# The Gram products of a later block, run directly behind the outputs of the delta rule

## The chip, the core and the metric

The kernel runs on one core of one Trainium2 chip. The metric is the device time of one execution in microseconds; smaller is better. The engines named below are PE (TensorE: matmuls, with PEld for its weight loads), DVE (VectorE), ACT (ScalarE) and SP (SyncE, which issues nearly all DMAs). Each engine works through its own list of instructions in order and waits at an instruction until what it needs is there.

## The reference

Two stages are fused: a delta-rule attention over 4 sequences, 8 heads, 768 tokens and a head dimension of 48, and an MLP on its output.

```python
k_n = k / (np.linalg.norm(k, axis=-1, keepdims=True) + 1e-06)
for t in range(S):
    y[:, :, t] = np.einsum('bhd,bhde->bhe', q[:, :, t], state)
    v_old = np.einsum('bhde,bhd->bhe', state, kt)
    state = state + bt[:, :, :, None] * np.einsum('bhd,bhe->bhde', kt, vt - v_old)
...
x = y, as 3072 tokens of 8 * 48 = 384 features
h = x @ w_in                      # 384 -> 2048
out = np.maximum(0.01 * h, h) @ w_out   # 2048 -> 384
```

Here `kt`, `vt` and `bt` are the key (normalised), value and step size of token t.

## The kernel before

**Blocks.** The 768 tokens of each sequence are cut into 12 blocks of 64. Inside a block the recurrence is replaced by matrix products and one triangular inverse; only the small state passes from block to block. For a block n there are these parts:

- `gram(n)`: the products of keys with keys and with queries. It loads the operands `kq` (four DMAs on SP, L267), starts the key lengths of the block before (`pn`, L530, copied to `nt` by ACT, L537), and then makes two groups of 16 matmuls each (`pg`, L287). A group fills two PSUM banks, b = 0 and b = 1; the operands of b = 0 lie on partitions 0 to 47, those of b = 1 from 64 on. The source goes through the two banks in alternation. ACT copies the key-key half of each bank to `gs` (L291), SP stores pieces of it to `gd` (L295), DVE masks the key-query half into `rq` (L302) and copies a corner to `gm` (L307), and SP loads `L` from `gd` (L310).
- `inv(n)`: an elimination by rows on DVE (`tmp` L351, `T` L356), some sixty pairs of small instructions per block, then a copy of `T` by ACT (L416), stores and loads through memory (`td`, `tt`, `sq`, `rt`) and the products `pz` and `pu` (L451).
- `solve(n)`: the steps that need the state: `pk` (L575), `pw` (L591), `pc` (L601), which makes the new state, and `py` (L611), whose copy `ys` (L613) is the block's output.
- `ffn(n)`: the MLP on the block's 256 tokens, in 16 f-steps. An f-step makes `ph` (nine matmuls, L670). ACT forms `gh` (L675) and rewrites `ph` in place (L676), DVE takes the difference `gl` (L678), and `po` (L660, six matmuls) of the f-step two before is added up. Two PSUM banks hold `ph`: f-steps of one parity share a bank and change between its halves. Behind the f-steps `columns` transposes the next block's output (`px`, L641) into `xh` and `xl` (L119, L120).

**What runs with what.** MLP block n is interleaved with `solve(n+1)`, `inv(n+2)` and `gram(n+3)`. `weave` goes through the f-steps of a block and calls the other parts' generators in windows of f-steps. The Gram of blocks 5 to 11 has the window 12 to 13: it is called in one piece in f-step 12, in MLP blocks 2 to 8.

**What sets the order.** From this source a scheduler makes one list of instructions per engine. `behind(name)` gives it one more edge: what is issued inside comes after the instruction that was last marked with that name. The products `pg` stand behind "ph". All products of `solve` and `gram` take their PSUM from one pool of four banks, in turn (`ps_a`, L68), so a product waits until the copies out of the bank's last use are done. `kq` has two buffers, one for each of a block's two groups.

Of the kernel before, what the change touches and what calls it, by code (L numbers as in the profile page):

```python
# [25 lines left out]
NGR = NSEQ // GS  # L26
# [5 lines left out]
P = 128  # L32
# [14 lines left out]
def delta_moe_kernel(ctx: ExitStack, tc, kq0, kqT, kv, qT, beta, cst, w_all, out, nblk):  # L47
# [208 lines left out]
            done.add((gram, n))  # L256
            yield

    def gram(n):
        need(sv, solve, n - Q_BUFS // NGR)  # L260
        kqs = []
        for g in range(NGR):
            t = sb.tile([P, GS, NPAIR, 2, C], F32, tag="kq", name=f"kq{n}_{g}", bufs=KQ_BUFS)
            kqs.append(t)
            with behind("kq"):
                for b in range(2):
                    nc.sync.dma_start(t[b * R0:b * R0 + D].rearrange("p s u x t -> p (s u x t)"), kqT[n, g, b])  # L267
        b0 = where[n][0]
        Lh[b0] = sb.tile([P, HC, HC], F32, tag="L", name=f"L{b0}", bufs=2)
        gd = dr.tile([64, HC, HC], F32, tag="gd", name=f"gd{n}")  # L270
        if n - 1 > 1 and where[n - 1][0] in nrm:
            with behind("ph"):
                lengths(n - 1)
        for g in range(NGR):
            kq = kqs[g]
            gs = sb.tile([P, 2, NPAIR, C], F32, tag="gs", name=f"gs{n}_{g}", bufs=2)
            if not g:
                gm[n] = sb.tile([P, GU, HC], F32, tag="gm", name=f"gm{n}", bufs=GM_BUFS)

            ps = [ps_a.tile([P, 512], F32, tag="a", name=f"pg{n}_{g}_{b}") for b in range(2)]  # L280
            pv = [x.rearrange("p (u x t) -> p x u t", u=NPAIR, x=2) for x in ps]
            for p in range(NPAIR):
                for c in range(2):
                    for b in range(2):
                        r = slice(b * R0, b * R0 + D)
                        with behind("ph") if n > 2 else nullcontext():
                            nc.tensor.matmul(ps[b][c * 64:(c + 1) * 64, p * 128:(p + 1) * 128],  # L287
                                             kq[r, c ^ b, p, 0], kq[r, c ^ b, p].rearrange("p x t -> p (x t)"),
                                             start=True, stop=True)
            for b in range(2):  # L290
                nc.scalar.copy(gs[:, b], pv[b][:, 0])  # L291
            for c in range(2):
                for e in range(2):
                    a = e * HS + g * GH + c * GU
                    nc.sync.dma_start(  # L295
                        gd[a:a + GU].rearrange("l j i -> j l i"),
                        gs[c * 64 + e * HC:c * 64 + (e + 1) * HC].rearrange("p b u t -> p (b u) t")[:, :, e * HC:(e + 1) * HC])
            qa = of("q", n, g)
            for b in range(2):
                for c in range(2):  # L300
                    r = slice(c * 64, (c + 1) * 64)
                    nc.vector.tensor_tensor(  # L302
                        qa[DN, c, b * NPAIR:(b + 1) * NPAIR], pv[b][r, 1],
                        tri[r].rearrange("p (o t) -> p o t", o=1).broadcast_to([C, NPAIR, C]), ALU.mult)
            for c in range(2):
                k = 2 * g + c
                nc.vector.tensor_copy(gm[n][k * HC:(k + 1) * HC].rearrange("p (b u) t -> p b u t", b=2), gs[c * 64:c * 64 + HC, :, :, HC:])  # L307
            if g == NGR - 1:
                for r in range(2):
                    nc.sync.dma_start(Lh[b0][r * 64:(r + 1) * 64].rearrange("l j i -> l (j i)"), gd.rearrange("l j i -> l (j i)"))  # L310
                done.add((gram, n))
            yield
# [232 lines left out]
    def solve(n):  # L545
        b = where[n][0]
        need(iv, inv, b)
        if n not in nts:
            with behind("po"):
                lengths(n)  # L550
        nt = nts.pop(n)

        def load(g):
            merge_z(n, g, tv(n, g))
            if n:
                fetch(n, g)

        def tie(g):
            merge_u(n, g, tv(n, g))

        def heads(rows):

            return ((c, u, slice(c * 64, c * 64 + rows)) for u in range(GU) for c in range(2))

        def out_of(x, g, w):
            p = ps_a.tile([P, 512], F32, tag="a", name=f"{x}{n}_{g}")
            return p[:, 0:GU * w].rearrange("p (u t) -> p u t", u=GU)

        def kt(g):

            t, k, v = tv(n, g), of("k", n, g), of("v", n, g)
            if n:
                pv = out_of("pk", g, C)
                for c, u, r in heads(D):
                    nc.tensor.matmul(pv[r, u], k[DN, c, u], t[DN, c, u // NPAIR, u % NPAIR], start=True, stop=True)  # L575
                for c in range(2):
                    nc.scalar.mul(t[UP, c], pv[c * 64:c * 64 + D].rearrange("p (y v) t -> p y v t", y=2), -1.0)  # L577
            if not n:
                return
            for s in range(GS):  # L580
                us = slice(s * NPAIR, (s + 1) * NPAIR)
                with behind("gl"):
                    nc.vector.tensor_tensor(
                        v[DN, :, us], v[DN, :, us],
                        nt[DN, g, :, us].rearrange("p h (u o) -> p h u o", o=1).broadcast_to([C, 2, NPAIR, D]), ALU.mult)

        def step_w(g):
            t, v = tv(n, g), of("v", n, g)
            pv = out_of("pw", g, D)
            for c, u, r in heads(C):  # L590
                nc.tensor.matmul(pv[r, u], t[:, c, u // NPAIR, u % NPAIR], v[:, c, u], start=True, stop=True)  # L591
            for c in range(2):
                d = nc.scalar.copy(v[DN, c], pv[c * 64:c * 64 + C])  # L593
            mark["rv"] = d.ins

        def step_s(g):
            k, v, v1 = of("k", n, g), of("v", n, g), of("v", n + 1, g)
            pv = out_of("pc", g, D)
            for c, u, r in heads(D):
                with nullcontext() if n else behind("px"):  # L600
                    nc.tensor.matmul(pv[r, u], k[:, c, u], v[:, c, u], start=True, stop=True)  # L601
            for c in range(2):
                nc.scalar.copy(v1[UP, c], pv[c * 64:c * 64 + D])  # L603

        def step_y(g):

            qa, v = of("q", n, g), of("v", n, g)
            pv = ps_a.tile([P, 512], F32, tag="a", name=f"py{n}_{g}")
            for c, u, _ in heads(C):
                s = c ^ (u // NPAIR)  # L610
                nc.tensor.matmul(pv[s * C:(s + 1) * C, u * D:(u + 1) * D], qa[:, c, u], v[:, c, u], start=True, stop=True)  # L611
            ys[n, g] = y = sb.tile([P, DO], F32, tag="ys", name=f"ys{n}_{g}", bufs=3)
            mark["ys"] = nc.scalar.copy(y, pv[:, 0:DO]).ins  # L613

        stages = [(0, load), (1, tie), (LD, kt), (LD + 1, step_w), (LD + 2, step_s), (LD + 2, step_y)]
        if n in (0, nblk - 1):
            stages.remove((LD + 2, step_s))
        for s in range(NSLOT):
            for g in range(NGR):
                for at, stage in stages:  # L620
                    if at == s:
                        stage(g)
            if s == NSLOT - 1:
                done.add((solve, n))
                if n == 0:
                    columns(0)
                    yield
                    for g in range(NGR):
                        step_s(g)
            yield  # L630
# [19 lines left out]
    def ffn(n):  # L650
# [5 lines left out]
        def second(f, gh, gl, tiles=range(NTB)):  # L656
            for t in tiles:
                ts_ = slice(t * P, (t + 1) * P)
                for k, (a, w) in enumerate(((gh, wo[0]), (gh, wo[1]), (gl, wo[0]))):
                    i = nc.tensor.matmul(  # L660
                        po[t][:, :DO], a[:, ts_], w[f],
                        start=(f == 0 and k == 0), stop=(f == NFC - 1 and k == 2))
            mark["po"] = i.ins

        for f in range(NFC):
            ph = hbank[f % 2][:, f // 2 % 2]
            k = 0
            for cc in range(NCC):
                for a, e in ((wi[0], 0), (wi[0], 1), (wi[1], 0)):
                    i = nc.tensor.matmul(ph, a[f][:, cc * P:(cc + 1) * P], x[cc][e], start=(k == 0), stop=(k == 3 * NCC - 1))  # L670
                    k += 1
            mark["ph"] = i.ins
            gh = sb.tile([P, TB], F32R, tag="gh", name=f"gh{n}_{f}", bufs=FB)
# [70 lines left out]
    for n in range(nblk):  # L744
# [1 line left out]
        weave(NF, (ff, NF, 0, NF), (wg, NFC * (n == 0), 0, WB),  # L746
              (lw, (NFC - 1) * (n == 0), 1 - LL, NFC - LL), (sv, (NS + (n == 0)) * (n + 1 < nblk), *SV[min(n, 3)]),
              (iv, NI * (n + 2 < nblk), *IV[min(n, 3)]), (gg, NGR * (n < 3), *GG[min(n, 2)]),
              (gg, NGR * (1 < n < nblk - 3), 12, 13))


WAHEAD, WEARLY = 4, 8
# [4 lines left out]
LL, AG = 2, 6  # L757
SV = (0, 9), (3, 11), (2, 11), (2, 11)
PD, FB = 2, 3


def _layout(inputs):
# [62 lines left out]
```

## Time and profile before

| | us |
|---|---|
| median of 3 runs | 645.03 (643.98 to 645.08) |
| profiled execution, its time | 645.91 |
| its span, first to last instruction | 644.1 |
| PE busy | 600.8 |
| DVE busy | 444.5 |
| ACT busy | 332.2 |

A timeline row is: start in us, length in us, engine, line and operation, output and inputs, count, and in brackets the idle time before it with what ended it. A chain row is: start, length, engine, tile and line; the chain is the work that ended last, followed back through what released each step. In a row of a window the length of the stretch is followed by the busy time of PE, PEld, DVE, ACT and POOL with their instruction counts, the granted TensorE clock as a share of full speed, the busy share of the DMA engines and GB/s. Many matmuls of the source are two instructions each in the trace, and a few of their records are missing.

### The profile page before, as it was taken

To read this page: it belongs to the slowest core of one execution; us is meant where nothing else is said; L and a number is where in the kernel's file an instruction comes from. 1 tells how busy PE (TensorE), PEld (TensorE's weight loads), DVE (VectorE), ACT (ScalarE), POOL (GpSimd) and SP (SyncE) were. 2 spreads that over 40 slices of the span, in tenths; PEclk is the share of its full clock that TensorE was granted. 3 is DMA by queue.
4 is the path that set the end of the run, shared out by engine and by line. 5 is a ranking of instruction groups with operands and counts; after the bars stand their busy time and mean duration, and the time that the engine had idled before them with its cause. 6 is when DMAs were issued, how large, how long until landed. Compare 5 with 4: busy or idle time off the path is not lost.

```text
span 644.1 us, 19692 instructions
## 1 busy us (share of the span) xinstructions
PE 600.8 (93%) x7710; PEld 560.3 (87%) x7710; DVE 444.5 (69%) x1996; ACT 332.2 (52%) x856; POOL 10.7 (2%) x17
## 2 busy tenths in 40 slices
PE   4287999989999989999999999999999999999996
PEld 4275888989889888999999999999999999999996
DVE  3999999988645959759749749659669659221221
ACT  3465998524645435635545546545545545444322
POOL 6000000000000000000000000000000000000000
PEclk9987999989999989999999999999999999999999
DMA  4992962153165641561561570660660640400101
GB/s 115 295 261 85 252 234 76 26 108 51 30 126 103 134 98 28 103 120 37 101 110 49 114 139 6 118 138 4 121 135 4 126 81 16 79 16 1 26 1 26
DMA packets 124573, 59.52 MB, mean 92 GB/s; under 512 B 111424, under 2 KB 114624, under 8 KB 124480
## 3 DMA queue, kind: packets, MB, share of 16 engines
q1 hardware_dynamic: 123904, 57.54, 40.5%
q8 instruction: 61, 1.00, 0.6%
q10 hardware_dynamic: 576, 0.72, 0.5%
q14 instruction: 32, 0.26, 0.1%
HBM read 46.96 MB, written 11.27 MB: 90 GB/s over the span
## 4 chain that ended last, share of the span: by engine, by line
PE 80%; DVE 7%; DMA 7%; ACT 4%; issue 2%; DVEq 0%; SPq 0%; ACTq 0%
PE ph L670 32%; PE po L660 30%; PE pk L575 3%; PE pw L591 3%; PE pg L287 3%; PE py L611 3%; PE pc L601 2%; DMA kq<-in_kqT 2%; DMA rv<-in_kv 2%; PE px L641 1%; DMA wr<-in_w_all 1%; DVE cg L151 1%; DVE tmp L351 1%; DVE T L356 1%; DVE rq L302 1%
## 5 line engine op out<-in xcount | busy, mean ns | idle before, releaser
L670 PE MATMUL ph<-xh,w 128*128 128x256 f32 x1152 | 247.5, 290 | 5.4 <-DVE gl L678 4.4
L670 PEld LDWEIGHTS ph<-xh,w 128*128 128x128 f32 x1152 | 192.6, 191 | 14.0 <-DVE gl L678 5.7
L660 PE MATMUL po<-w,gh 128*128 128x384 f32 x768 | 188.0, 343 | 3.2 <-ACT gh L675 3.2
L678 DVE TENSOR_TENSOR gl<-ph,gh 128x256 fp32r<-128x256 f32 x192 | 80.2, 421 | 140.5 <-ACT ph L676 138.3
L670 PE MATMUL ph<-xl,w 128*128 128x256 f32 x576 | 163.0, 284 | 1.0 <-DVE xl L120 1.0
L675 ACT ACTIVATE gh<-ph 128x256 fp32r<-128x256 f32 x192 | 73.7, 384 | 170.8 <-PE ph L670 169.0
L660 PEld LDWEIGHTS po<-w,gh 128*128 128x128 f32 x768 | 133.4, 189 | 8.1 <-ACT gh L675 5.3
L660 PE MATMUL po<-w,gl 128*128 128x384 f32 x384 | 115.2, 340 | 0.0
L351 DVE TENSOR_TENSOR tmp<-T,L 128x60 f32<-128x60 f32 (+35 forms) x661 | 112.4, 207 | 0.9
L356 DVE TENSOR_TENSOR T<-T,tmp 128x60 f32<-128x60 f32 (+35 forms) x661 | 111.9, 207 | 0.9
L670 PEld LDWEIGHTS ph<-xl,w 128*128 128x128 f32 x576 | 109.9, 191 | 1.8 <-DVE xl L120 1.5
L676 ACT ACTIVATE ph<-ph 128x256 f32<-128x256 f32 x192 | 73.2, 381 | 0.0
L660 PEld LDWEIGHTS po<-w,gl 128*128 128x128 f32 x384 | 66.8, 190 | 0.1
L302 DVE TENSOR_TENSOR rq<-pg,csb 64x256 f32<-64x256 f32 x80 | 33.8, 423 | 12.6 <-ACT gs L291 11.3
L593 ACT COPY rv<-pw 64x384 f32<-64x384 f32 x48 | 22.7, 473 | 17.9 <-PE pw L591 17.1
L577 ACT ACTIVATE rt<-pk 48x512 f32<-48x512 f32 x44 | 26.1, 592 | 10.0 <-PE pk L575 9.3
L603 ACT COPY rv<-pc 48x384 f32<-48x384 f32 x44 | 20.8, 474 | 13.8 <-PE pc L601 13.5
L591 PEld LDWEIGHTS pw<-rv,rt 128*64 128x64 f32 x768 | 25.1, 145 | 3.1 <-ACT ph L676 2.3
L611 PE MATMUL py<-rv,rq 128*64 128x48 f32 x768 | 27.6, 227 | 0.0
L591 PE MATMUL pw<-rv,rt 128*64 128x48 f32 x768 | 26.8, 230 | 0.0
L120 DVE TENSOR_TENSOR xl<-px,xh 128x256 fp32r<-128x256 f32 x36 | 14.2, 419 | 17.8 <-ACT xh L119 17.8
L611 PEld LDWEIGHTS py<-rv,rq 128*64 128x64 f32 x768 | 25.7, 143 | 0.2 <-ACT ph L676 0.2
(96 smaller groups left out, 557.5 us busy)
## 6 DMA issues: line engine op xcount, KB each, us to landing
wr<-in_w_all SPq DMA_DIRECT2D x16, 768.0 KB, 7.6
kq<-in_kqT SPq DMA_DIRECT2D x40, 192.0 KB, 5.1
L<-gd SPq DMA_DIRECT2D x20, 256.0 KB, 4.0
rk<-in_kv SPq DMA_DIRECT2D x24, 192.0 KB, 3.7
rv<-in_kv SPq DMA_DIRECT2D x24, 192.0 KB, 4.6
rq<-in_qT SPq DMA_DIRECT2D x24, 192.0 KB, 4.5
out<-ob SPq DMA_DIRECT2D x46, 96.0 KB, 2.9
gd<-gs SPq DMA_DIRECT2D x80, 32.0 KB, 2.0
```

The costliest lines, as they stand in the source:

```text
L302: nc.vector.tensor_tensor(qa[DN, c, b * NPAIR:(b + 1) * NPAIR], pv[b][r, 1], tri[r].rearrange("p (o t) -> p o t", o=1).broadcast_to([C, NP ...
L351: nc.vector.tensor_tensor(tv, t[:, :, j:j + 1].broadcast_to([P, k, w]), L[:, j, j + 1:].rearrange("p (o w) -> p o w", o=1).broadcast_to([P ...
L356: mark["steps"] = nc.vector.tensor_tensor(t, t, tv, ALU.subtract).ins
L577: nc.scalar.mul(t[UP, c], pv[c * 64:c * 64 + D].rearrange("p (y v) t -> p y v t", y=2), -1.0)
L591: nc.tensor.matmul(pv[r, u], t[:, c, u // NPAIR, u % NPAIR], v[:, c, u], start=True, stop=True)
L593: d = nc.scalar.copy(v[DN, c], pv[c * 64:c * 64 + C])
L611: nc.tensor.matmul(pv[s * C:(s + 1) * C, u * D:(u + 1) * D], qa[:, c, u], v[:, c, u], start=True, stop=True)
L660: i = nc.tensor.matmul(po[t][:, :DO], a[:, ts_], w[f], start=(f == 0 and k == 0), stop=(f == NFC - 1 and k == 2))
L670: i = nc.tensor.matmul(ph, a[f][:, cc * P:(cc + 1) * P], x[cc][e], start=(k == 0), stop=(k == 3 * NCC - 1))
L675: nc.scalar.activation(gh, ph, AF.Prelu, alpha=0.01)
L676: i = nc.scalar.activation(ph, ph, AF.Prelu, alpha=0.01)
L678: i = nc.vector.tensor_tensor(gl, ph, gh.bitcast(F32), ALU.subtract)
```

## The change

The operands of `gram(n+2)` are now loaded by a function of their own, `grab`, which `solve(n)` calls at its step `pk`, group 1. The Gram is called in the window of f-step 10 and no longer 12. Its last product is marked "pg", and the first product of each `ph` group and of each `po` group stands behind that mark.

```diff
+    held = {}
+    def grab(n):
+        held[n] = []
         for g in range(NGR):
             t = sb.tile([P, GS, NPAIR, 2, C], F32, tag="kq", name=f"kq{n}_{g}", bufs=KQ_BUFS)
-            kqs.append(t)
+            held[n].append(t)
             with behind("kq"):
                 for b in range(2):
                     nc.sync.dma_start(t[b * R0:b * R0 + D].rearrange("p s u x t -> p (s u x t)"), kqT[n, g, b])
+    def gram(n):
+        need(sv, solve, n - Q_BUFS // NGR)
+        if n not in held:
+            grab(n)
+        kqs = held.pop(n)
...
                         with behind("ph") if n > 2 else nullcontext():
-                            nc.tensor.matmul(ps[b][c * 64:(c + 1) * 64, p * 128:(p + 1) * 128],
+                            i = nc.tensor.matmul(ps[b][c * 64:(c + 1) * 64, p * 128:(p + 1) * 128],
...
+            if n > 4:
+                mark["pg"] = i.ins
...
         def kt(g):
+            if g and 2 < n < nblk - 2:
+                grab(n + 2)
...
         def second(f, gh, gl, tiles=range(NTB)):
...
+                    with behind("pg") if not k else nullcontext():
...
         for f in range(NFC):
...
+                    with behind("pg") if not k else nullcontext():
...
-              (gg, NGR * (1 < n < nblk - 3), 12, 13))
+              (gg, NGR * (1 < n < nblk - 3), RUN, RUN + 1))
+RUN = 10
```

What moves is best seen in the lists of MLP block 7, in which the Gram of block 10 runs. On PE, at the end of f-step 10, there stood before (`po7_1` is the second half of `po` in block 7; `w10` and `gh7_10` belong to f = 10; `pg10_0_0` is group 0, bank 0):

```order
L660 MATMUL po7_1_7125<-w10_1313,gh7_10_7554 128x384 x2
L660 MATMUL po7_1_7125<-w10_1313,gl7_10_7555 128x384
L530 MATMUL pn9_7731<-csb_74,sq8_7178 64x32
L287 MATMUL pg10_0_0_7737<-kq10_0_7723 64x128
L287 MATMUL pg10_0_1_7738<-kq10_0_7723 64x128
```

The last two rows repeat eight times, then group 1 follows in the same manner. Now PE has, at the end of the steps of `solve(8)`, ahead of `ph` of f = 11:

```order
L613 MATMUL pc8_1_7609<-rv1_85,rk1_77 48x48 x16
L623 MATMUL py8_1_7628<-rv1_85,rq1_79 64x48 x16
L540 MATMUL pn9_7661<-csb_74,sq8_7178 64x32
L295 MATMUL pg10_0_0_7667<-kq10_0_7410 64x128 x8
L295 MATMUL pg10_0_1_7668<-kq10_0_7410 64x128 x8
L295 MATMUL pg10_1_0_7698<-kq10_1_7413 64x128
L295 MATMUL pg10_1_1_7699<-kq10_1_7413 64x128
```

The run stands two f-steps earlier, directly behind `py`; group 0 goes through its banks one after the other, and only group 1 (the last two rows, eight times) alternates. All seven runs have this form. Further on, `po` of f = 11 has its first two matmuls ahead of `ph` of f = 13, and the six transposes stand in five places where they stood in two.

On ACT the list at the same place was:

```order
L613 COPY ys8_1_7639<-py8_1_7622 128x384
L675 ACTIVATE gh7_11_7662<-ph1_73 128x256
L676 ACTIVATE ph1_73<-ph1_73 128x256
L416 COPY T8_7174<-T8_7174 128x16x32
L675 ACTIVATE gh7_12_7700<-ph0_72 128x256
L676 ACTIVATE ph0_72<-ph0_72 128x256
L537 COPY nt9_7733<-pn9_7731 64x32
L291 COPY gs10_0_7735<-pg10_0_0_7737 128x256
```

and is now:

```order
L625 COPY ys8_1_7645<-py8_1_7628 128x384
L547 COPY nt9_7663<-pn9_7661 64x32
L301 COPY gs10_0_7665<-pg10_0_0_7667 128x256
L426 COPY T8_7174<-T8_7174 128x16x32
L301 COPY gs10_0_7665<-pg10_0_1_7668 128x256
L301 COPY gs10_1_7697<-pg10_1_0_7698 128x256
L301 COPY gs10_1_7697<-pg10_1_1_7699 128x256
L689 ACTIVATE gh7_11_7739<-ph1_73 128x256
```

The copy of `T` now stands between the first and the second `gs`, in MLP blocks 4 to 8; in block 3 it stands ahead of the first, and in block 2 behind all of them. On DVE, the list at the end of the elimination was:

```order
L356 TENSOR_TENSOR T8_7174<-T8_7174,tmp8_30_0_7948 128x8
L678 TENSOR_TENSOR gl7_11_7663<-ph1_73,gh7_11_7662 128x256
L678 TENSOR_TENSOR gl7_12_7701<-ph0_72,gh7_12_7700 128x256
L302 TENSOR_TENSOR rq0_78<-pg10_0_0_7737,csb_74 64x256 x2
L302 TENSOR_TENSOR rq0_78<-pg10_0_1_7738,csb_74 64x256 x2
L307 COPY gm10_7736<-gs10_0_7735 32x256 x2
```

and is now:

```order
L366 TENSOR_TENSOR T8_7174<-T8_7174,tmp8_30_0_7948 128x8
L312 TENSOR_TENSOR rq0_78<-pg10_0_0_7667,csb_74 64x256 x2
L312 TENSOR_TENSOR rq0_78<-pg10_0_1_7668,csb_74 64x256 x2
L317 COPY gm10_7666<-gs10_0_7665 32x256 x2
L312 TENSOR_TENSOR rq1_79<-pg10_1_0_7698,csb_74 64x256 x2
L312 TENSOR_TENSOR rq1_79<-pg10_1_1_7699,csb_74 64x256 x2
L317 COPY gm10_7666<-gs10_1_7697 32x256 x2
L692 TENSOR_TENSOR gl7_11_7740<-ph1_73,gh7_11_7739 128x256
```

`gl` of f = 11 and f = 12 stood ahead of the Gram's instructions and now stands behind all of them. In block 2 the elimination is not over at this place, and its rows are mixed with the Gram's instructions there.

More of the change, by code (lines that the diff above doesn't have):

```diff
@@ L257, in first @@
             yield
-    def gram(n):
-        need(sv, solve, n - Q_BUFS // NGR)
-        kqs = []
+    held = {}
+    def grab(n):
+        held[n] = []
         for g in range(NGR):
             t = sb.tile([P, GS, NPAIR, 2, C], F32, tag="kq", name=f"kq{n}_{g}", bufs=KQ_BUFS)
-            kqs.append(t)
+            held[n].append(t)
             with behind("kq"):
@@ L286, in gram @@
                         with behind("ph") if n > 2 else nullcontext():
-                            nc.tensor.matmul(ps[b][c * 64:(c + 1) * 64, p * 128:(p + 1) * 128],
-                                             kq[r, c ^ b, p, 0], kq[r, c ^ b, p].rearrange("p x t -> p (x t)"),
-                                             start=True, stop=True)
+                            i = nc.tensor.matmul(ps[b][c * 64:(c + 1) * 64, p * 128:(p + 1) * 128],
+                                                 kq[r, c ^ b, p, 0], kq[r, c ^ b, p].rearrange("p x t -> p (x t)"),
+                                                 start=True, stop=True)
+            if n > 4:
+                mark["pg"] = i.ins
             for b in range(2):
@@ L659, in second @@
                 for k, (a, w) in enumerate(((gh, wo[0]), (gh, wo[1]), (gl, wo[0]))):
-                    i = nc.tensor.matmul(
-                        po[t][:, :DO], a[:, ts_], w[f],
-                        start=(f == 0 and k == 0), stop=(f == NFC - 1 and k == 2))
+                    with behind("pg") if not k else nullcontext():
+                        i = nc.tensor.matmul(
+                            po[t][:, :DO], a[:, ts_], w[f],
+                            start=(f == 0 and k == 0), stop=(f == NFC - 1 and k == 2))
             mark["po"] = i.ins
@@ L669, in ffn @@
                 for a, e in ((wi[0], 0), (wi[0], 1), (wi[1], 0)):
-                    i = nc.tensor.matmul(ph, a[f][:, cc * P:(cc + 1) * P], x[cc][e], start=(k == 0), stop=(k == 3 * NCC - 1))
+                    with behind("pg") if not k else nullcontext():
+                        i = nc.tensor.matmul(ph, a[f][:, cc * P:(cc + 1) * P], x[cc][e], start=(k == 0), stop=(k == 3 * NCC - 1))
                     k += 1
```

## The prediction

> **What bounds the kernel now.** I read the page's busy line and chain shares first, then the stretches block by block, then the chain of waits inside one block. An f-step below is one `ph` group and one `po` group; `gl11` is the `gl` of f=11 of its block.
>
> ```profile
> core 0: 644.1 us, clock 0.984
> PE 600.8 (93%) x7710; PEld 560.3 (87%) x7710; DVE 444.5 (69%) x1996; ACT 332.2 (52%) x856; POOL 10.7 (2%) x17
> PE 80%; DVE 7%; DMA 7%; ACT 4%; issue 2%; DVEq 0%; SPq 0%; ACTq 0%
> 398.22:445.39 47.17, 46.87 (x602) 44.04 (x604) 34.09 (x173) 24.25 (x64) 0.00 (x0) 1.00 0.44 88
> 445.39:492.33 46.94, 46.64 (x602) 44.03 (x604) 34.14 (x173) 24.16 (x64) 0.00 (x0) 1.00 0.43 89
> 205.00:232.00 27.00, 24.60 (x363) 23.19 (x362) 26.21 (x153) 11.18 (x31) 0.00 (x0) 0.94 0.45 104
> ```
>
> The last three lines are stretches: length, then busy time of PE, weight load, DVE, ACT and POOL. The second of them is MLP block 7, typical of blocks 3 to 8: PE is busy 46.64 of 46.94 us. Such a block gets shorter only if PE has less to do, and longer by whatever PE is made to wait or do more. The third stretch, in MLP block 2, is different: DVE is busy 26.21 of 27.00 us, so DVE sets the pace there.
>
> The chain of waits through block 7, from the last `py` to the transposes:
>
> ```profile
> 452.21 0.93 PE py L611 x32
> 453.14 1.27 PE ph L670 x9
> 454.41 1.06 PE po L660 x6
> 455.46 1.07 PE ph L670 x9
> 456.54 1.05 PE po L660 x6
> 457.59 0.17 PE pn L530
> 457.76 1.83 PE pg L287 x59
> 459.60 1.28 PE ph L670 x9
> 460.87 1.06 PE po L660 x6
> 461.93 1.08 PE ph L670 x9
> 463.01 1.06 PE po L660 x6
> 464.07 0.11 PE px L641
> 464.18 0.70 PE po L660 x4
> 464.88 0.55 PE px L641 x5
> ```
>
> Every piece is PE, end to start. The first `ph` behind small matmuls (`py`, `pg`) takes 1.27 or 1.28 us, one behind a `po` 1.07: leaving a stretch of small tiles costs PE about 0.21.
>
> **The change part by part.** It moves 7 Gram runs (blocks 5 to 11, in MLP blocks 2 to 8). I work block 7 out from the end of `py`, 453.14, to the start of `ph` of f=14, today 461.93: 8.79 us.
>
> *The move itself.* `pn` and `pg` now follow `py` directly; one exit from small tiles goes. In order: 0.17 + 1.83 + 1.27 + 1.06 + 1.07 + 1.05 + 1.07 + 1.06 = 8.58, which is 0.21 less. That is all the gain PE can make: the matmuls are the same. The transposes come in five groups where there were two, but 0.11 alone and 0.55 for five is the same each: nothing.
>
> *The Gram's order.* Today the matmuls of its two banks, which read partitions 0 to 47 and 64 to 111, alternate. In the changed program the first 16 of bank 0 (8 in the source, two instructions each) go together, then 16 of bank 1, and only the other 32 alternate. The trace has both forms on PE, the second in the Gram of block 4:
>
> ```profile
> 457.66 1.94 PE L287 MATMUL pg<-kq 48*64 48x128 f32 x61
> 186.29 1.06 PE L287 MATMUL pg<-kq 48*64 48x128 f32 x15
> 188.07 1.96 PE L287 MATMUL pg<-kq 48*64 48x128 f32 x48
> 68.97 1.59 PE L287 MATMUL pg<-kq 48*64 48x128 f32 x32
> ```
>
> One matmul lasts 0.27, so the starts of the first row are (1.94 - 0.27)/60 = 0.028 apart, those of the second (1.06 - 0.27)/14 = 0.056. The third holds 16 of bank 1 and 32 alternating ones: 1.69 less 32 x 0.028 leaves 0.79 for 15 steps, 0.053. The fourth, 32 in two runs of 16, is cheaper: (1.59 - 0.27)/31 = 0.043. The price of the new order is 32 x (0.056 - 0.028) = 0.90 by the second row, 32 x (0.043 - 0.028) = 0.48 by the fourth, which stands apart, early in the program. I take 0.87, between the second and third. PE has no idle time to hide it. By PE alone `ph` of f=14 then starts 8.58 + 0.87 = 9.45 behind `py`, 0.66 later than now.
>
> The Trainium skill, "TensorE: Matmul & The Clock Gate", Part 3, says that a weight load overlaps matmuls in flight only where the row group differs; the trace agrees, 0.028 against 0.056, and without that rule one might have taken the fourth row, 0.39 us a run less. The Trainium skill, "TensorEngine Tiling (Array Packing)", Key Properties, says that a change of tiling mode drains TensorE, and by it `py` to `pn` still pays a switch, as I assume; if that one were free, the sum would be 0.1 us a run lower, 0.7 in all.
>
> *What DVE is given first.* The move brings the Gram's work on DVE forward too: 8 `rq` and 4 `gm` instructions now stand between the end of the elimination and `gl11`, where today `gl11` and `gl12` come ahead of them.
>
> ```profile
> 454.53 0.17 DVE L356 TENSOR_TENSOR T<-T,tmp 128x8 f32<-128x8 f32 x1
> 459.17 1.75 DVE L302 TENSOR_TENSOR rq<-pg,csb 64x256 f32<-64x256 f32 x4 [1.41 <-ACT gs L291]
> 460.95 0.58 DVE L307 COPY gm<-gs 32x256 f32<-32x256 f32 x2
> 461.54 1.73 DVE L302 TENSOR_TENSOR rq<-pg,csb 64x256 f32<-64x256 f32 x4
> 463.28 0.58 DVE L307 COPY gm<-gs 32x256 f32<-32x256 f32 x2
> 463.90 0.76 DVE L678 TENSOR_TENSOR gl<-ph,gh 128x256 fp32r<-128x256 f32 x2
> 453.24 0.48 ACT L613 COPY ys<-py 128x384 f32<-128x384 f32 x1
> 455.03 1.08 ACT L416 COPY T<-T 128x512 f32<-128x512 f32 x1
> 458.76 0.65 ACT L291 COPY gs<-pg 128x256 f32<-128x256 f32 x2 [0.72 <-PE pg L287]
> 416.70 0.42 DVE L678 TENSOR_TENSOR gl<-ph,gh 128x256 fp32r<-128x256 f32 x1
> 417.18 0.19 PEld L670 LDWEIGHTS ph<-xh,w 128*128 128x128 f32 x1 [0.25 <-DVE gl L678]
> ```
>
> The burst takes 463.90 - 459.17 = 4.73. Who waits for a late `gl11`: `po` of f=11, and, by the last two rows (block 6), the next `ph` in the same PSUM bank too, though it fills the other half: `ph` of f=15 stood still until `gl13` had ended at 417.12. So `gl11` now holds `ph` of f=13. On ACT the new order is `ys`, `nt`, first `gs`, the `T` copy, three `gs`. The elimination ends at 454.70; the first `rq` pair runs at once, since bank 0 ends near 454.2 and its `gs` (half of the 0.65 above and the start of one) near 454.6; the `T` copy runs from 454.76 to 455.84, the second `gs` to 456.21, and the rest of the burst, 4.73 - 0.87 = 3.86, from 456.25 to 460.11; `gl11` ends at 460.54 and `ph` of f=13 cannot start before 460.60. PE gets there at 453.14 + 0.17 + 2.70 (1.83 + 0.87) + 1.27 + 1.06 + 1.07 + 1.05 = 460.46, and the first two of the six `po` of f=11 (0.35 of 1.06), which now stand ahead of it, make it 460.81. So with 0.87 PE is the later one by 0.2 and DVE's stall is covered; with 0.48 the start is 460.60, DVE's. From there to `ph` of f=14 go 1.07 and the other four `po`, 0.71: 1.78: **0.66 later, or 0.45**.
>
> Blocks 4 to 8: 5 x 0.66 = 3.30. Block 3: there the `T` copy stands ahead of all four `gs`. By block 7's times the burst then runs whole from 456.25 to 460.98, `gl11` ends at 461.41, `ph` of f=13 starts at 461.47 and f=14 at 463.25: +1.32. Block 6 loses its old stall at f=15, the 47.17 against 46.94 above: -0.23. Block 2 remains:
>
> ```profile
> 226.71 0.42 DVE L678 TENSOR_TENSOR gl<-ph,gh 128x256 fp32r<-128x256 f32 x1
> 227.19 0.38 PE L670 MATMUL ph<-xh,w 128*128 128x256 f32 x1 [2.40 <-DVE gl L678]
> ```
>
> PE waits 2.40 there for `gl13` behind burst and elimination. DVE's work in this stretch stays the same and now holds `gl11`, so the stall moves two f-steps up. I take +0.2; it could give back up to 2.4 if elimination rows let `gl` through earlier, or cost 1.5 if PE's spare time comes too late.
>
> *The loads and queues.* Where the four `kq` loads stand in SP's queue hardly changes, only that they are issued at the `pk` step. The eight `gd` stores now stand ahead of the loads of the next inverse.
>
> ```profile
> 474.19 3.06 SPq L267 DMA_DIRECT2D kq<-in_kqT  x4
> sq<-tt SPq DMA_DIRECT2D x40, 32.0 KB, 2.1
> 475.86 0.65 PE L451 MATMUL pz<-sq,gm 128*32 128x128 f32 x16
> ```
>
> The loads issued from 474.19 are read some 30 us later, by the Gram one block (46.94) behind that of 457.76. The `sq` loads, issued from 469 on today, land in 2.1, and `pz` reads them at 475.86: some 4 us of slack against eight stores of about 0.5 each that were mostly ahead of them already. Nothing.
>
> **Sum.** 3.30 + 1.32 - 0.23 + 0.2 = +4.6. The profiled execution took 645.91 (span 644.1 and 1.8 around it), the median of the runs is 645.03 (643.98 to 645.08). Its sum is 650.5; against the median I predict **649.6**. A measurement of this kernel can tell about 0.2%, 1.3 us, from no change.
>
> **Rivals.**
>
> *B: both prices are low.* The single-bank runs cost 0.48 as at 68.97, and `gl11` is out before PE needs it. Then a run costs 0.48 - 0.21 = 0.27, seven 1.9, less 0.23: **646.7**. For it: that row. Against it: the other two rows, nearer in time and in order, and DVE's chain, which would have to end 0.2 us sooner than I worked out.
>
> *C: faster.* `ph` of f=13 follows only its own half of the bank (`gl9`), so the burst on DVE is covered, and what happens is the saved exit. It decides if the Gram costs less than 0.21 extra; at no extra, seven times -0.21 and -0.23 give **643.3**. For it: the code addresses halves. Against it: the wait at 417.18 and the two forms of `pg`. The Trainium skill's drain rule above would leave this number as it is, and by a free entry it would be 642.6.
>
> *D: the Gram starts late.* Its four banks are those that `pc`, `py` and `pn` have just left: ACT's copies must end first (`ys` from 453.24 to 453.72, then `nt`). I see them free 0.4 us or more ahead of need. If `pg` starts late enough that its first `gs` ends near 455.4 and not 454.6, the `T` copy behind it, the second `gs` and the burst shift by up to 0.75 and `ph` of f=13 with them: five blocks more by about 0.7, **653**. For it: ACT's queue is in order and has this all at once. Against it: the slack.
>
> **Chances.** My forecast 0.65, B 0.13, C 0.09, D 0.13. The forecast alone spans 647.5 (0.45 in five blocks and block 2 giving back 1) to 651.5 (a price of 0.90 and block 2 costing 1.5). The range reaches to B and D: 645.0 to 653.3. Faster by over 0.2%: C, and a part of block 2's bound, 0.10. Within 0.2%: the low half of B and the edge of C, 0.12. Slower: 0.78.
>
> **What would show it.** Right: `pg` takes about 2.7 us behind `pn`, with PE busy; the first `ph` behind `pg` takes 1.27, no `ph` behind `po` does; blocks 4 to 8 last about 47.6; `ph` of f=13 shows no wait on `gl` or one of 0.2; in block 3 it waits about 0.7. Wrong: `pg` at 1.83 (C), a wait of `pg` on ACT's copies (D), blocks 4 to 8 at 47.2 (B), or a wait on `gl` above 0.5 in these blocks, which would mean that DVE's chain is later than I worked out.

## The result

The changed kernel takes 648.66 us (646.96 to 649.79, 4 runs), the kernel before in the same rounds 645.06 (643.98 to 645.83, 4 runs): 1.0055 times, 95% interval 1.0028 to 1.0082. A second set of rounds gave 648.30 against 644.83, 1.0048 (1.0031 to 1.0065). It is slower by about half a per cent; 649.6 was predicted. Of the runs below, one of ten of the kernel with two edits, at a granted clock of 0.759, took 741.70 and is left out of its median.

The page of the changed kernel, lines that answer to those shown of before:

```profile
core 0: 645.1 us, clock 0.984
PE 602.8 (93%) x7710; PEld 562.2 (87%) x7710; DVE 443.9 (69%) x1996; ACT 331.9 (51%) x856; POOL 10.7 (2%) x17
PE 75%; DVE 17%; issue 3%; ACT 3%; DMA 2%; SPq 0%; DVEq 0%; ACTq 0%
```

This execution took 646.96, the lowest of the four. On the chain DVE has risen from 7% to 17%, but 42 us of that rise stand in the first 100 us, ahead of all that moves, and 15 us between 205 and 271, in MLP blocks 2 and 3. From there on the chain has 0.1 us of DVE in both kernels: a wait as short as those of blocks 5 to 8 below doesn't show in these shares.

Where the time goes is seen best by blocks. The end of the last `py` in the timeline of PE cuts the span into stretches; the one named after MLP block n goes from there to the same point of block n+1, with block n's Gram run in it. (The `py` of block n+1 runs in MLP block n; so the expectations below call stretches 2 to 8 "from py of block 3 to py of block 10".) Only column 1 is named after the block in which it ends: it goes from the last `py` in MLP block 0 to that in MLP block 1. What lies between columns 1 and 2, 38.11 before and 37.88 changed, is left out. In us:

| | 1 | 2 | 3 | 4 | 5 | 6 | 7 | 8 | sum of 2 to 8 |
|---|---|---|---|---|---|---|---|---|---|
| before | 72.16 | 52.09 | 46.94 | 46.94 | 46.95 | 47.17 | 46.94 | 46.94 | 333.97 |
| changed | 70.66 | 52.55 | 48.07 | 47.26 | 47.41 | 47.41 | 47.42 | 47.40 | 337.52 |
| difference | -1.50 | +0.46 | +1.13 | +0.32 | +0.46 | +0.24 | +0.48 | +0.46 | +3.55 |

The seven stretches that the change touches lose 3.55, near the 3.60 by which the medians differ. The profiled executions differ by only 1.0: column 1, in which both kernels have the same instructions on PE, ACT and DVE as far as the traces show, gives back 1.50, and the parts not in the table another 1.0. The last section comes back to column 1. The other runs have no such table, so that 3.55 and 3.60 are so close may be chance; in a second pair of profiled executions, below, the seven stretches lose 4.23, and the executions differ by 2.3.

Block 7 of the changed kernel, the chain of waits from the last `py` on:

```profile
452.11 0.93 PE py L623 x32
453.05 0.17 PE pn L540
453.21 2.33 PE pg L295 x61
455.55 1.26 PE ph L684 x9
456.81 1.05 PE po L673 x6
457.86 1.07 PE ph L684 x9
458.94 1.40 PE po L673 x8
460.34 1.25 PE ph L684 x9
461.59 0.71 PE po L673 x4
```

`pg` takes 2.33 where it took 1.83: 0.50 more, which I take as the price of the Gram's order. Only one `ph` behind small tiles is left, 455.55. The third `ph`, f=13 at 460.34, takes 1.25 and not 1.07, because PE waits in front of it. The weight load of that group, and what DVE and ACT do until then:

```profile
460.25 0.19 PEld L684 LDWEIGHTS ph<-xh,w 128*128 128x128 f32 x1 [0.23 <-DVE gl L692]
...
454.43 0.17 DVE L366 TENSOR_TENSOR T<-T,tmp 128x8 f32<-128x8 f32 x1
454.63 0.86 DVE L312 TENSOR_TENSOR rq<-pg,csb 64x256 f32<-64x256 f32 x2
455.95 0.86 DVE L312 TENSOR_TENSOR rq<-pg,csb 64x256 f32<-64x256 f32 x2 [0.46 <-ACT gs L301]
...
459.78 0.76 DVE L692 TENSOR_TENSOR gl<-ph,gh 128x256 fp32r<-128x256 f32 x2
...
454.21 0.37 ACT L301 COPY gs<-pg 128x256 f32<-128x256 f32 x1 [0.39 <-PE pg L295]
454.63 1.07 ACT L426 COPY T<-T 128x512 f32<-128x512 f32 x1
455.50 0.96 ACT L301 COPY gs<-pg 128x256 f32<-128x256 f32 x3
```

DVE's chain is the one that the prediction worked out, 0.3 sooner: the first `rq` pair at once, then 0.46 of waiting for the second `gs`, which stands behind the `T` copy, and `gl11` out at 460.2. Some 0.1 of the 0.3 is an earlier `py`, and 0.2 is that the second `gs` starts 0.2 before the `T` copy ends (455.50 against 455.70), where the prediction put them end to end. PE came sooner still: its weight load stood ready at 460.02.

### The profile page after: what moved, and what is told of

It is laid out like the page before. It is cut to its first block, busy times and chain, and to the rows that moved or that the text cites. A ratio compares the mean times of both kernels' runs of the same rounds, so it can differ in the third digit from the quotient of the medians.

```text
span 645.1 us, 19658 instructions
## 1 busy us (share of the span) xinstructions
PE 602.8 (93%) x7710; PEld 562.2 (87%) x7710; DVE 443.9 (69%) x1996; ACT 331.9 (51%) x856; POOL 10.7 (2%) x17
## 4 chain that ended last, share of the span: by engine, by line
PE 75%; DVE 17%; issue 3%; ACT 3%; DMA 2%; SPq 0%; DVEq 0%; ACTq 0%
PE ph L684 30%; PE po L673 29%; DVE T L366 3%; DVE tmp L361 3%; PE pk L587 3%; PE pg L295 3%; PE pw L603 3%; PE py L623 2%; PE pc L613 2%; DVE rq L312 2%; DVE cg L151 1%; PE px L653 1%; DVE gl L692 1%; DMA wr<-in_w_all 1%; PE pz L461 1%
## 5 line engine op out<-in xcount | busy, mean ns | idle before, releaser
L673 PE MATMUL po<-w,gl 128*128 128x384 f32 x384 | 111.8, 338 | 0.0
L673 PEld LDWEIGHTS po<-w,gl 128*128 128x128 f32 x384 | 65.5, 188 | 0.1
L295 PE MATMUL pg<-kq 48*64 48x128 f32 x640 | 26.6, 274 | 0.0
```

The lines of the kernel that those rows point to most:

```text
L295: i = nc.tensor.matmul(ps[b][c * 64:(c + 1) * 64, p * 128:(p + 1) * 128], kq[r, c ^ b, p, 0], kq[r, c ^ b, p].rearrange("p x t -> p (x t)" ...
L673: i = nc.tensor.matmul(po[t][:, :DO], a[:, ts_], w[f], start=(f == 0 and k == 0), stop=(f == NFC - 1 and k == 2))
```

## The experiments

The theory after the result has three terms for a block: -0.21 for the saved exit from small tiles, +0.50 for the Gram's order, +0.18 for the wait of `ph` f=13 for `gl11`; together +0.47. The rivals give the loss to one of them alone. Stretches, measured as above:

| kernel | 1 | 2 | 3 | 4 | 5 | 6 | 7 | 8 | sum of 2 to 8 |
|---|---|---|---|---|---|---|---|---|---|
| T copy last | 70.66 | 51.99 | 47.23 | 47.21 | 47.22 | 47.22 | 47.22 | 47.22 | 335.31 |
| alternating | 70.64 | 52.10 | 48.19 | 48.31 | 48.29 | 47.70 | 47.52 | 47.52 | 339.63 |
| alternating, T copy last | 70.63 | 51.51 | 47.05 | 46.85 | 46.93 | 46.83 | 46.83 | 46.84 | 332.84 |
| the same, gm on GpSimd | 70.67 | 53.05 | 46.82 | 46.81 | 46.82 | 46.83 | 46.84 | 46.83 | 334.00 |
| single runs, old place | 72.16 | 51.92 | 47.44 | 47.44 | 47.45 | 47.41 | 47.45 | 47.45 | 336.56 |
| half runs, T copy last | 70.64 | 53.47 | 46.95 | 46.82 | 46.99 | 46.99 | 46.99 | 46.99 | 335.20 |
| changed, gm on GpSimd | 70.65 | 51.61 | 47.21 | 47.21 | 47.22 | 47.20 | 47.24 | 47.23 | 334.92 |
| loads alone | 72.17 | 52.56 | 46.94 | 46.95 | 46.95 | 47.11 | 46.95 | 46.94 | 334.40 |
| three edits, block 2 old | 72.15 | 50.90 | 46.82 | 46.82 | 46.82 | 46.84 | 46.84 | 46.85 | 331.89 |
| changed again | 70.62 | 53.33 | 48.07 | 47.29 | 47.41 | 47.43 | 47.45 | 47.43 | 338.41 |
| before again | 72.16 | 52.32 | 46.95 | 46.95 | 46.94 | 47.14 | 46.94 | 46.94 | 334.18 |

Stretches 3 to 8 repeat within 0.05 from one execution to the next. Stretch 2 doesn't, and stretch 1 has two values (last section); nothing below rests on these two unless it says so.

**The wait for `gl11`, taken away on ACT.**

```diff
-                nc.scalar.copy(gs[:, b], pv[b][:, 0])
+                mark["gs"] = nc.scalar.copy(gs[:, b], pv[b][:, 0]).ins
...
-                    nc.scalar.copy(Tt.rearrange("p i m -> p m i"), T)
+                    with behind("gs") if n > 3 else nullcontext():
+                        nc.scalar.copy(Tt.rearrange("p i m -> p m i"), T)
```

> The changed kernel with one edge more: ACT copies T only behind all four gs of the Gram. PE's list is the same as in the changed kernel. My theory: a block there is 0.46 us longer than before, made of -0.21 (one exit from small tiles saved), +0.50 (the Gram's first two banks one after the other) and about +0.18 (ph of f=13 waits for gl11, which stands behind the Gram's work on DVE, which waited 0.46 for the second gs behind the T copy). Then the wait at f=13 goes: gl11 ends near 459.7 of block 7 and PE comes at 460.0. Blocks 4 to 8 are +0.29 against before instead of +0.46, block 3 +0.3 instead of +1.13; from the end of py of block 3 to that of block 10 the kernel takes 335.9 (before 333.97, changed 337.52). Rival, the order of the Gram alone is the price and ACT's order matters nothing: 337.5 as it is, with block 3 still at +1.1.

Measured: 47.21 to 47.23 in blocks 3 to 8, +0.28, and the extra of block 3 is gone with it. A single run took 646.38 beside 645.41 for before. DVE has no hole in the burst any more, `gl11` is out at 460.0 and PE doesn't wait; `pg` still takes 2.33. The last two rows are the weight load of `ph` f=13 and, on the chain, its matmuls:

```profile
453.47 2.33 PE pg L295 x61
...
454.90 1.73 DVE L312 TENSOR_TENSOR rq<-pg,csb 64x256 f32<-64x256 f32 x4
...
459.60 0.80 DVE L693 TENSOR_TENSOR gl<-ph,gh 128x256 fp32r<-128x256 f32 x2
460.26 0.19 PEld L685 LDWEIGHTS ph<-xh,w 128*128 128x128 f32 x1
460.59 1.07 PE ph L685 x9
```

**The same wait, taken away on DVE.** The changed kernel with `gm` copied by GpSimd, nothing else:

```diff
-                nc.vector.tensor_copy(gm[n][k * HC:(k + 1) * HC]...
+                (nc.gpsimd if n > 4 else nc.vector).tensor_copy(gm[n][k * HC:(k + 1) * HC]...
```

> The changed kernel with the gm copies of blocks 5 to 11 on GpSimd; ACT's and PE's order of the Gram stay (T copy between the first and the second gs, group 0 one bank after the other). The burst on DVE is 1.16 shorter, though it still waits for the second gs. My theory: gl11 ends near 459.0 of block 7 where PE comes at 460.0, no wait at f=13, blocks 4 to 8 at 47.22 like those with the T copy last, block 3 as well. Rival, what was lost is not the wait for gl11: blocks stay at 47.4, block 3 at 48.07.

Measured: 47.20 to 47.24 in blocks 3 to 8; the single run took 644.49 beside 645.35. The second `gs` is waited for as in the changed kernel, and yet `gl11` ends two us ahead of need (`ph` f=13 starts at 459.27 here):

```profile
454.20 2.61 DVE L312 TENSOR_TENSOR rq<-pg,csb 64x256 f32<-64x256 f32 x6 [0.44 <-ACT gs L301]
456.84 0.42 DVE L692 TENSOR_TENSOR gl<-ph,gh 128x256 fp32r<-128x256 f32 x1
```

PE's list has moved too: transposes and the rest of `po` now stand ahead of `ph` f=13. They aren't needed for it: `gl11` ends 6.0 behind the end of `py`, and PE stood ready for it 7.0 behind in the changed kernel. Two edits on two engines remove the same 0.2 a block, so the wait for `gl11` is shown to be that term.

**The order made cheap, DVE's chain made late.** Both banks of each group in alternation again, by an edge from each product to the next:

```diff
-                        with behind("ph") if n > 2 else nullcontext():
+                        with behind("ph") if n > 2 else nullcontext(), behind("one") if n > 4 else nullcontext():
                             i = nc.tensor.matmul(...)
+                        if n > 4:
+                            mark["one"] = i.ins
```

> The changed kernel with both banks of every Gram group in alternation, as before the change. The scheduler then puts the T copy ahead of all four gs in blocks 3 to 8, as the changed kernel has it in block 3 alone. My theory, DVE's chain decides: pg takes 1.83 again and PE would come to ph of f=13 0.50 sooner, but the Gram's work on DVE starts only behind T copy and gs, gl11 ends some 0.85 later, and every block from 3 to 8 takes 48.0 to 48.2, as block 3 does in the changed kernel (48.07); from py of block 3 to py of block 10 about 341. Rival, the order of the Gram is the price: blocks at 46.8 to 46.9, 334 in all.

Measured: PE has less to do, and blocks 3 to 8 are slower than in the changed kernel, 287.5 us against 285.0; the single run took 649.09 beside 645.41 for before. In blocks 3 to 5 the stretch is 48.2 to 48.3, close to the changed kernel's block 3 (48.07). Block 3 here:

```profile
264.29 1.06 ACT L428 COPY T<-T 128x512 f32<-128x512 f32 x1 [0.52 <-DVE T L368]
265.38 1.20 ACT L303 COPY gs<-pg 128x256 f32<-128x256 f32 x4
...
265.79 1.73 DVE L314 TENSOR_TENSOR rq<-pg,csb 64x256 f32<-64x256 f32 x4 [1.53 <-ACT gs L303]
...
270.96 0.38 PE L686 MATMUL ph<-xh,w 128*128 128x256 f32 x1 [1.09 <-DVE gl L694]
```

The copy waits for the elimination, all four `gs` wait for the copy, DVE idles 1.53 and PE 1.09. Blocks 6 to 8 lose less than I expected (47.5 to 47.7): there transposes and the rest of `po` stand ahead of `ph` f=13, and PE waits 0.4 to 0.6.

**Both edits, and `gm` on GpSimd as well.**

> Both of the edits: banks in alternation, and the T copy behind all four gs. My theory: PE comes to ph of f=13 near 459.5 of block 7, and DVE, which goes from the last T at 454.63 through the whole burst without a gap, lets gl11 go at about 459.75, so that a wait of 0.2 to 0.3 is left and the saved exit is eaten up: blocks at 46.9 to 47.0, as before the change; from py of block 3 to py of block 10 about 334.3, the time within 0.2% of before. Rival, no wait is left: 0.21 less in each block, 332.5 from py to py.

> Both of the edits and a third: the gm copies of blocks 5 to 11 go from DVE to the idle GpSimd. That takes 4 x 0.29 = 1.16 from the burst on DVE, so that gl11 ends near 458.6, ahead of need. My theory: no wait for gl is left in blocks 3 to 8, only the saved exit remains, blocks at 46.73; block 2, where DVE sets the pace, gains up to 1; from py of block 3 to py of block 10 about 332.0, the time 642.5 to 643.5, 0.2 to 0.4% under before. Rival, GpSimd's copies are slow enough or disturb DVE so much that DVE's rows get longer: blocks at 47 or more.

Measured for the two edits: 0.9982 of before (0.9969 to 0.9996), 643.63 against 645.41; with the third 0.9973 (0.9961 to 0.9985), 643.91. Blocks 3 to 8 take 46.81 to 47.05. My theory expected a wait of 0.2 to 0.3 with two edits, and there is none in five of the six blocks (block 3 has one, 0.26): the scheduler had put transposes and `po` ahead of `ph` f=13, and `gl11` ends at 458.1, a full us before it. With the third edit no such wait is left in any of the six, and blocks 6 to 8 are no shorter for it; the time misses the 642.5 to 643.5 that I expected. Block 2 gained nothing in the profiled execution (53.05), but has twice the lowered clock there that before has, so its own gain stays open. The rival is not right either: the gain is 0.11 and not 0.21. The rows of the two edits tell where the other 0.10 is:

```profile
451.27 0.17 PE pn L543
451.44 1.93 PE pg L295 x64
453.37 1.27 PE ph L687 x9
...
457.68 0.76 DVE L695 TENSOR_TENSOR gl<-ph,gh 128x256 fp32r<-128x256 f32 x2
...
459.19 1.06 PE ph L687 x9
```

The same alternating Gram takes 1.93 behind `py` and 1.83 behind `po`; in single runs it takes 2.33 at either place. Why was not tried.

**The order alone, and the length of a run.** First the kernel before with its Gram in the changed order (`b` the outer loop in group 0, with the chain of edges), then the changed kernel with the T copy last and group 0 in four runs of 8:

```diff
+            if n > 4 and not g:
+                pcb = [(p, c, b) for b in range(2) for p in range(NPAIR) for c in range(2)]
...
+                pcb = [(2 * h + p, c, b) for h in range(2) for b in range(2) for p in range(2) for c in range(2)]
```

> The kernel before with one thing of the change: in the Gram of blocks 5 to 11 the two banks of group 0 are filled one after the other and no longer in alternation, at the old place behind po of f=10. It prices the order alone. My theory now: the two runs of 16 overlap where they meet, so that pg takes 0.40 more (2.33 against 1.93 in the two runs with the T copy last), PE has no idle time, and blocks 3 to 8 take 47.34 (block 6: 47.5); from py of block 3 to py of block 10 336.8 (before: 333.97). Rival, my prediction's price of 0.87: blocks at 47.8, 340.1.

> The changed kernel with the T copy last (blocks of 47.22), and group 0 of the Gram in four runs of 8 instructions, banks 0, 1, 0, 1, in the place of two runs of 16. It has as many instructions that do not alternate with their neighbour's bank inside runs, but twice the seams. My theory, loads and matmuls of two banks run together for some instructions around each seam, and only the middle of a long run pays 0.055 an instruction: the price falls from 0.40 to under 0.15, blocks at 46.85 to 46.97. Rival, each instruction in a run pays the same: blocks stay at 47.2.

Measured: 47.44 at the old place, +0.50 on 46.94 and not 0.40 or 0.87; the single runs took 647.7 and 644.74 beside 645.35. With half runs `pg` falls to what alternation takes behind `py`. The Gram of block 10 at the old place, before (first) and in single runs; then behind `py`, alternating (from the kernel with two edits) and in half runs, with PE's wait there:

```profile
457.66 1.94 PE L287 MATMUL pg<-kq 48*64 48x128 f32 x61
...
458.47 2.44 PE L288 MATMUL pg<-kq 48*64 48x128 f32 x63
...
451.37 2.00 PE L295 MATMUL pg<-kq 48*64 48x128 f32 x63
...
452.25 2.02 PE L296 MATMUL pg<-kq 48*64 48x128 f32 x63
458.96 0.19 PEld L688 LDWEIGHTS ph<-xh,w 128*128 128x128 f32 x1 [0.21 <-DVE gl L696]
```

Half runs leave almost nothing of the price, so the price is not one per instruction: it is paid in the middle of a long run. What is left in those blocks, 46.99 (46.97 was the upper end expected), holds a wait of 0.2 for `gl11` again, since PE now comes sooner; in block 4, without it, the stretch is 46.82. The changed kernel's own `pg` shows the seams. Slices of 0.1 us; behind the slice's length stand the busy time and, in brackets, the number of `pg` matmuls that touch the slice on PE, then of weight loads on PEld:

```profile
453.45:453.55 0.10, 0.10 (x6) 0.10 (x4) 0.00 (x0) 0.00 (x0) 1.00 1.21 471
453.65:453.75 0.10, 0.10 (x9) 0.10 (x9) 0.00 (x0) 0.00 (x0) 1.00 1.63 440
453.95:454.05 0.10, 0.10 (x11) 0.10 (x4) 0.00 (x0) 0.00 (x0) 1.00 0.81 246
454.75:454.85 0.10, 0.10 (x14) 0.10 (x10) 0.10 (x1) 0.00 (x0) 1.00 0.00 0
```

Inside a run (first and third line) 4 loads touch a slice; where bank 0's run meets bank 1's it is 9, and 10 in this slice of the alternating part (8 in most). So work of the other bank runs along with a run's ends. The Trainium skill, "TensorE: Matmul & The Clock Gate", Part 3, says that a weight load is pulled ahead of matmuls in flight where its row group differs, out of a reorder window 64 deep. The trace agrees with the pull-ahead (9 loads against 4); how deep it reaches, no run here shows, except that runs of 8 are covered and the middle of runs of 16 is not. This reach across a seam is what the prediction left out when it charged every instruction of a run.

**The loads alone.** The `kq` loads at the `pk` step, the Gram at f-step 12, no edges on `ph` and `po`:

```diff
-RUN = 10
+RUN = 12
...
-                    with behind("pg") if not k else nullcontext():
+                    if True:
```

> The loads of kq at the pk step alone: the Gram stays in the window of f-step 12, and no ph or po stands behind it. My theory: the kernel before, 46.94 a block (block 6 at 47.17) and 334.0 from py of block 3 to py of block 10. Rival, the loads collide with others or come too late for the Gram: a wait of pg on kq, or blocks that differ by more than 0.05.

Measured: before's blocks, 645.36 beside 645.35. The loads are free and bring nothing.

**The best of them, and the two kernels again.**

```diff
-              (gg, NGR * (1 < n < nblk - 3), RUN, RUN + 1))
+              (gg, NGR * (1 < n < nblk - 3), RUN + 2 * (n == 2), RUN + 1 + 2 * (n == 2)))
...
-            if n > 4:
+            if n > 5:
                 mark["pg"] = i.ins
```

> The kernel with all three edits (banks in alternation, T copy behind the gs, gm copies on GpSimd), with the Gram run of block 5, in MLP block 2, back at its old place in the window of f-step 12; the runs of blocks 6 to 11 stay behind py. My theory: blocks 3 to 8 at 46.83 as with the three edits; in block 2, where DVE sets the pace, the burst without gm is 1.16 shorter, so that block falls from 52.1 to about 51.2; from py of block 3 to py of block 10 332.1, the time 0.2 to 0.4% under before. Rival, block 2 is not bound to the burst's place or length: 52 to 53 as before.

> The changed kernel once more, in rounds against the one before. My theory: from py of block 3 to py of block 10 between 337.0 and 338.0 in the profile, blocks 4 to 8 at 47.26 to 47.42 again, the time 3.0 to 4.2 over before; in MLP block 1, ahead of any difference in the lists, 70.65 again if that stretch belongs to the program and not to chance. Rival, the loss by block differs from one execution to the next, and the sum above was chance.

> The kernel before once more, one look. From py of block 3 to py of block 10 it should take 333.7 to 334.5, blocks 3 to 8 46.94 (47.1 to 47.2 in block 6). The open question is the stretch of MLP block 1, ahead of any difference in the lists: 72.16 before, 70.65 in the changed kernel. If the lowered clock there belongs to the program, it is 72.16 again; if it belongs to chance, 70.65.

Measured: 642.90 against 644.83, 0.9969 (0.9957 to 0.9982): faster than before and than the changed kernel; from the 0.9973 with the Gram of block 5 behind `py` too it can't be told apart. Blocks 3 to 8 take 46.82 to 46.85. Block 2 came out at 50.90, near what was expected, but not for the reason given: PE waits 2.35 for `gl13` there, as it waited 2.40 before, and what is missing is the lowered clock behind that wait. Windows of before and of this kernel; the third number from the end is the granted clock:

```profile
228.00:234.00 6.00, 6.00 (x33) 5.90 (x32) 4.67 (x31) 3.12 (x8) 0.00 (x0) 0.72 0.26 50
...
228.00:234.00 6.00, 5.44 (x33) 4.34 (x31) 3.10 (x17) 3.00 (x8) 0.00 (x0) 1.00 0.43 62
225.94 0.39 PE L687 MATMUL ph<-xh,w 128*128 128x256 f32 x1 [2.35 <-DVE gl L695]
```

Six us at 0.72 are worth 1.7 us at full clock, more than the 1.2 by which the stretch is shorter. So against before the runs don't show that block 2 gains from the place of its Gram. Three kernels with that Gram behind `py` have no lowered clock in block 2 either (T copy last, alternating with T copy last, changed with gm on GpSimd); they take 51.51 to 51.99 there, this one 50.90. That speaks for the old place in block 2, but from one execution each, of kernels that differ in other edits too. The changed kernel repeated its stretches 3 to 8 within 0.03, and 337.0 to 338.0 in all was missed with 338.41, by block 2 alone; before repeated its own.

## Why the prediction held

The direction, the size (+3.6 measured, +4.6 predicted) and the range held. By its steps:

- **The saved exit**, -0.21. Right as a difference of the two wholes: single runs at the old place cost +0.50, in the new place with no wait +0.28, so the place is worth 0.22. With the banks alternating it is worth 0.11. What a switch from `py` to `pn` costs by itself, 0.1 in the prediction, no run shows.
- **The Gram's order**, +0.87 from bounds of 0.48 and 0.90. The term that was mis-sized: at the old place it measures 0.50 (2.44 against 1.94), at the new place 0.40 (2.33 against 1.93 on the chain). So the sum of place and order, +0.28, is measured; how it splits depends on where the order is priced. The row at 68.97 gave 0.48, and I set it aside for standing early in the program. It had what the row at 186.29 lacked: two runs of 16 that meet. The 0.053 to 0.056 an instruction holds inside a run, away from where it meets another. The trace of before also had a whole Gram of this kind, which the prediction doesn't use: block 3's, whose weight loads show an alternating part (mostly 8 or 9 to a slice of 0.1 us) and single runs (4 to a slice from 126.9 to 127.3). It takes 0.44 more than the 1.94 of the alternating one:

```profile
126.10 2.38 PE L287 MATMUL pg<-kq 48*64 48x128 f32 x61
```

- **DVE's chain.** Right in its order, its parts and its bank: `ph` f=13 cannot start before `gl11` ends. I took 0.87, by which PE is the later one, and gave 0.45 a block for the low price, where DVE is. The second case came: 0.46 to 0.48 in blocks 5, 7 and 8, with 0.18 of it the wait; by the prediction's own times a price of 0.48 gives 460.60 - 460.42 = 0.18. That this size fits is luck in part: `gl11` ended 0.34 sooner than worked out, and PE needed it 0.3 sooner, since the weight load of a `ph` starts 0.3 before the matmuls ahead of it end (460.26 against 460.59 in the run with the T copy last). In block 4 PE doesn't wait, and the loss is 0.32.
- **Block 3**: +1.13 for +1.32, with a wait of 0.56 on PE for one of about 0.7:

```profile
270.75 0.39 PE L684 MATMUL ph<-xh,w 128*128 128x256 f32 x1 [0.56 <-DVE gl L692]
```

- **Block 6** loses its old stall, as said: +0.24, 0.23 less than its neighbours.
- **Block 2**: +0.46 for +0.2, +1.0 in the second pair of executions. The stall moved up and stayed (2.60 at 220.24 in place of 2.40 at 227.19). All four executions have a lowered clock there, worth 1.7 us each, so the clock doesn't make the difference; but the kernel with the loads alone, whose Gram stays at the old place, took 52.56 with the same clock. So neither the size nor the sign of this term is settled.
- **Loads and queues**: nothing. The run with the loads alone shows it for the loads, and for the queue `pz` waits for no load in blocks 3 to 8. The 4 us of slack were counted from the first `sq` loads, though: before, the last one is issued at 472.3 and such a load lands 3.0 later, half a us ahead of `pz`.
- **The rivals.** D's mechanism, a late Gram, didn't occur: the first `gs` ended at 454.58 where 454.6 was worked out. B's low price came true and its early `gl11` did not. C's saved exit without any price took two more edits, and then gave half.

Of the signs named, the wait of 0.2 and the one long `ph`, behind `pg` (1.26), came; `pg` at 2.7 and blocks at 47.6 did not (2.33, and 47.3 to 47.4, between the forecast and B's 47.2). That the total came out near is in part the cancelling of two errors in blocks 4 to 8: 0.37 too much for the order, 0.18 too little for the wait.

## What to carry to other kernels

A block of work that moves brings its consumers along on the other engines: here the matmuls cost PE little at the new place, but DVE's and ACT's share of them came ahead of a copy and of `gl`, and PE waited for those. When a scheduler reorders a run of small matmuls, price the order from a row with the same neighbours at both ends, because runs on different partitions overlap where they meet. And once one term is taken away, look for the next that was covered by it: cheaper matmuls, with the order that the scheduler then gave ACT, made this kernel slower.

## What the runs showed that I had not expected

The clock behind a wait of about two us is not the same in all programs. In MLP block 1 every kernel has, as far as the traces show, the same instructions on PE, ACT and DVE, and PE waits 2.02 for `gl`. Before and in the changed kernel, with the granted clock as third number from the end of the windows:

```profile
135.65 0.49 PE L670 MATMUL ph<-xh,w 128*128 128x256 f32 x1 [2.02 <-DVE gl L678]
133.00:139.00 6.00, 3.98 (x18) 3.66 (x17) 5.80 (x32) 0.66 (x2) 0.00 (x0) 0.73 0.70 163
...
134.67 0.39 PE L684 MATMUL ph<-xh,w 128*128 128x256 f32 x1 [2.02 <-DVE gl L692]
133.00:139.00 6.00, 4.33 (x30) 4.33 (x31) 5.91 (x39) 1.32 (x4) 0.00 (x0) 1.00 0.67 157
```

The lowered clock costs the stretch 1.5 us (72.16 against 70.66). In the five profiled executions of programs whose Gram of block 5 is at the old place it was there each time (72.15 to 72.17), in the eight with that Gram behind `py` never (70.62 to 70.67), though that Gram comes some 75 us later. The Trainium skill, "TensorE: Matmul & The Clock Gate", Part 1, says that the clock follows the activity in windows of 3.4 us that run free of the kernel's start; by that rule it should be chance, and 5 of 5 against 0 of 8 doesn't look like it. The length agrees: the three slices of 2 us from 134 on have a granted clock of 0.94, 0.50 and 0.70 in before, together 3.4 us at 0.50. At other places the drop does come and go: near 177 it is in three of the thirteen executions, of both groups. What decides it in block 1 stays open. It takes 1.5 us from the difference of the two profiled executions; whether it does so in the other runs behind the medians, whose traces aren't here, isn't known.
